# Half-tile K transposes on VectorE and small operations moved to GpSimd, in a cached-attention and MLP decode kernel

## The chip, the cores and the metric

The kernel runs on one core of a Trainium2 chip. The metric is the device time of one execution in microseconds (us); quoted times are medians of the runs of one kernel. The profile is of one such execution; its span is about 2 us shorter than the time. Engines are named as in the profile: PE is TensorE, PEld its weight loads, DVE is VectorE, ACT is ScalarE, POOL is GpSimd, SP the engine that issues the loads. The granted clock is the TensorE clock that the profile shows as granted, as a share of full speed.

## The reference, cut to what matters

```python
# x: (4, 1, 576) bf16; 32 query heads, 16 K/V heads, head size 128;
# attention over the last W = 2048 of 8192 cached keys
def reference(A_x, A_k_cache, A_v_cache, A_wq, A_wo, B_x, B_w1, B_w2, B_w3, B_w4):
    xn = layernorm(A_x)
    q = (xn @ A_wq)                                  # 2 query heads share one K/V head
    p = softmax(q @ k_window.T * 128 ** -0.5)
    attention = (p @ v_window).reshape(4, 1, 4096) @ A_wo
    # for a sequence of one token, the shifted mixer of the MLP branch adds nothing
    mlp = xn + gelu(layernorm(xn) @ B_w3) @ B_w4
    return A_x + attention + mlp
```

The work is small and the data large: for each of 16 K/V heads a K tile and a V tile of 2 MB (4 batch rows, 2048 keys, 128 channels, bf16), plus wq, wo, w3 and w4. Together the profile counts 87.17 MB on the load queue.

## The kernel before

A K tile arrives with keys on partitions, while the scores need channels there. DVE transposes it, seen as int32 (two bf16 channels at once), a quarter tile per instruction. Then PE multiplies; the softmax chain of the head before runs interleaved:

```python
def k_transpose(h, s):                     # s = 0..3, a quarter of the K tile of head h
    src = kv_tiles["K", h][:].bitcast(I32)[:, s * SC:(s + 1) * SC, :].rearrange("p c (ib i) -> p ib c i", i=QD)
    kt = ktp.tile([P, 2, SC, QD], I32, tag="kt")          # pool of 3 buffers
    nc.vector.transpose(out=kt[:], in_=src)
    kts[h, s] = kt

def sm_max(h):                             # maximum of the scores of head h
    mx = small.tile([P, 1], F32, tag="mx")
    nc.vector.reduce_max(out=mx[:], in_=S_ps[h][:], axis=AX.X)
    dm = small.tile([P, NG], BF16, tag="dm")
    nc.vector.tensor_scalar(out=dm[:], in0=sel_g[:], scalar1=mx[:, 0:1], scalar2=None, op0=ALU.mult)
    st["dm", h] = dm

def sm_maxT(h):                            # PE gathers the maxima over partitions: tile mg
    mg = ps_m.tile([NJ, NG], F32, tag="m", name="mg")
    nc.tensor.matmul(out=mg[:], lhsT=sel_jb[:], rhs=st.pop(("dm", h))[:], start=True, stop=True)
...
for t in range(Hkv):                       # hm, hv, hf, hp: heads t-1, t-2, t-3, t-4
    for s in range(NSL):                   # NSL = 4
        ...
        n = t * NSL + s + 1
        if n < Hkv * NSL:
            k_transpose(*divmod(n, NSL))   # the next quarter
        if s == 0:
            if hm >= 0:
                sm_max(hm)
            ...
            k_mask(t)
        elif s == 1 and hm >= 0:
            sm_maxT(hm)
        ...
        if hv >= 0:
            pv(hv, s)                      # probabilities times V, of head t-2
        k_scores(t, s)
```

So on PE's list stand, per head: mask, PV and scores (quarter 0), then **mg**, which needs dm, then PV and scores of quarter 1, and so on. PE takes its list in order: when dm is late, everything behind mg waits.

The loads share six K/V buffers. w4 comes last, in six pieces:

```python
W4_PIECES = [0, 10, NFH, NF - 6, NF - 2, NF - 1, NF]      # NFH = 18, NF = 36 blocks
...
mlp_out(*pieces[0]); ...; mlp_out(*pieces[1]); o_proj(hl)  # hl: the last head
mlp_out(*pieces[2]); mlp_out(*pieces[3])
... # copy one accumulator out, then pieces 4 and 5, the sum, the store
```

## Time and profile before

| | before |
|---|---|
| time, median of the first 3 runs (range) | 212.07 us (211.9 to 212.22) |
| span of the profiled run | 210.2 us |
| busy: PE, DVE, ACT, POOL | 147.2, 120.1, 33.9, 2.8 us |
| load queue, share of 16 engines' span | 97.5% |

Lines of the page of the kernel before: the busy time of the engines; then, over 40 equal slices of the span, the busy share of the DMA engines in tenths and the GB/s; then the load queue with packets, MB and share.

```profile
PE 147.2 (70%) x941; PEld 62.4 (30%) x955; DVE 120.1 (57%) x217; ACT 33.9 (16%) x64; POOL 2.8 (1%) x15
...
DMA  7999999999999999999999999999999999999991
GB/s 281 418 399 430 421 430 435 427 430 436 436 442 414 426 433 420 446 424 433 436 421 433 430 420 437 433 433 422 433 426 430 422 442 433 421 436 426 421 414 60
...
q1 hardware_dynamic: 6640, 87.17, 97.5%
```

No engine is close to full, and the DMA row is at 9 everywhere but in the first and the last slice. The kernel is bound by loading; there is no slice in which a faster engine would let loads start earlier.

Groups of DVE instructions (line, engine, operation, tile; busy us and mean ns of one; idle of DVE before them and what ended it), kernel before: the transposes, the maximum, and the product dm.

```profile
L225 DVE STREAM_TRANSPOSE kt<-kn 128x1024 int32<-128x1024 int32 x64 | 76.3, 1216 | 11.1 <-DMA kn<-in_A_k_cache_dram 10.8
L344 DVE TENSOR_REDUCE mx<-S 128x1 f32<-128x512 f32 x16 | 10.5, 657 | 1.3 <-PE S L338 1.3
...
L346 DVE TENSOR_SCALAR dm<-sel_g,mx 128x16 bf16<-128x16 bf16 x16 | 3.7, 231 | 0.6
```

What PE waited for, kernel before (us in total, times, longest us):

```profile
PE O L390 <- DMA vn<-in_A_v_cache_dram: 37.5, 10, 14.1
...
PE mg L351 <- DVE dm L346: 3.5, 3, 2.6
...
PE acc L183 <- DMA w_sb<-in_B_w_dram: 1.9, 1, 1.9
```

PE waits mostly for V tiles, hardly ever for dm. The last line is the slack of the compute: near the end PE has done everything that stands before this piece of w4 and waits 1.9 us for it. The same place in the timeline (start us, us, engine, line, what; in brackets the idle time before it and what ended it):

```profile
202.83 0.29 PE L183 MATMUL acc_odd<-wo_sb,op 128*8 128x288 bf16 x1
205.01 0.28 PE L183 MATMUL acc<-w_sb,gT 128*8 128x288 bf16 x1 [1.89 <-DMA w_sb<-in_B_w_dram]
```

### The profile page before, as it was taken

What the parts mean: (1) busy time and instruction counts of PE and PEld (TensorE: products, weight loads), DVE (VectorE), ACT (ScalarE), POOL (GpSimd) and SP (SyncE); (2) the same over time, 40 slices, a digit from 0 to 9 for tenths busy, and PEclk for the clock granted to TensorE, in tenths of its full rate; (3) what the DMA queues carried; (4) which work ended last, traced back from release to release, by engine and by line L of the source; (5) the groups of instructions that cost most, each with busy time, mean ns of one, the idle gap of its engine ahead of it and who ended that gap; (6) DMA issues with size and microseconds to landing.
All of it is one profiled execution on the core that took longest, in us unless ns stands there. A gap on an engine that the chain in (4) does not pass through costs nothing.

```text
span 210.2 us, 2389 instructions
## 1 busy us (share of the span) xinstructions
PE 147.2 (70%) x941; PEld 62.4 (30%) x955; DVE 120.1 (57%) x217; ACT 33.9 (16%) x64; POOL 2.8 (1%) x15
## 2 busy tenths in 40 slices
PE   0395694789394008849699689997883956988954
PEld 0132231224131002314154234343431321543533
DVE  4832999267831082637603879898578381593220
ACT  7603100021111000202012211220211020202300
POOL 4010000000000000000000000000000000000000
PEclk9998599589979555979699969999999695899999
DMA  7999999999999999999999999999999999999991
GB/s 281 418 399 430 421 430 435 427 430 436 436 442 414 426 433 420 446 424 433 436 421 433 430 420 437 433 433 422 433 426 430 422 442 433 421 436 426 421 414 60
DMA packets 6659, 87.32 MB, mean 415 GB/s; under 512 B 748, under 2 KB 1016, under 8 KB 1400
## 3 DMA queue, kind: packets, MB, share of 16 engines
q1 hardware_dynamic: 6640, 87.17, 97.5%
q8 instruction: 7, 0.11, 0.2%
q14 instruction: 4, 0.03, 0.0%
q10 hardware_dynamic: 8, 0.00, 0.0%
HBM read 87.17 MB, written 0.00 MB: 415 GB/s over the span
## 4 chain that ended last, share of the span: by engine, by line
DMA 65%; PE 22%; DVE 8%; issue 2%; ACT 1%; SPq 1%; DVEq 0%
DMA w_sb<-in_B_w_dram 33%; DMA vn<-in_A_v_cache_dram 26%; PE S L338 9%; DMA wq_sb<-in_A_wq_dram 6%; DVE kt L225 4%; PE O L390 3%; PE g_ps L456 2%; PE acc L183 2%; PE q_ps L285 2%; PE oT L403 1%; DVE mx L344 1%; PE S L360 1%; DVE qz L317 1%; PE gT_ps L468 1%; ACT q_sb L296 1%
## 5 line engine op out<-in xcount | busy, mean ns | idle before, releaser
L225 DVE STREAM_TRANSPOSE kt<-kn 128x1024 int32<-128x1024 int32 x64 | 76.3, 1216 | 11.1 <-DMA kn<-in_A_k_cache_dram 10.8
L338 PE MATMUL S<-kt,qz 128*128 128x512 bf16 x242 | 76.1, 437 | 5.2 <-DVE kt L225 3.1
L390 PE MATMUL O<-vn,PT 128*32 128x512 bf16 x256 | 27.9, 434 | 38.7 <-DMA vn<-in_A_v_cache_dram 37.5
L338 PEld LDWEIGHTS <-qz 128*128 128x128 bf16 x256 | 21.8, 104 | 42.0 <-issue 26.2
L366 ACT ACTIVATE E<-S 128x512 bf16<-128x512 f32 x16 | 9.5, 597 | 119.8 <-PE S L360 119.8
L390 PEld LDWEIGHTS <-PT 128*32 128x32 bf16 x256 | 7.3, 95 | 47.0 <-DVE kt L225 25.2
L372 DVE STREAM_TRANSPOSE PT<-E 128x512 bf16<-128x512 bf16 x16 | 11.4, 710 | 15.1 <-ACT E L366 15.1
L356 DVE TENSOR_REDUCE nm<-mg 8x1 bf16<-8x16 f32 x16 | 2.3, 146 | 23.0 <-PE mg L351 22.9
L397 ACT ACTIVATE O_sb<-O,rd 128x512 f32<-128x512 f32 x16 | 11.0, 686 | 16.2 <-issue 11.0
L344 DVE TENSOR_REDUCE mx<-S 128x1 f32<-128x512 f32 x16 | 10.5, 657 | 1.3 <-PE S L338 1.3
L413 DVE TENSOR_REDUCE on<-oT 128x8 bf16<-128x128 f32 x16 | 4.5, 280 | 11.1 <-PE oT L403 11.1
L403 PE MATMUL oT<-ident_w,O_sb 128*128 128x128 f32 x64 | 10.6, 291 | 0.2 <-issue 0.2
L403 PEld LDWEIGHTS oT<-ident_w,O_sb 128*128 128x128 f32 x64 | 8.6, 153 | 4.6 <-issue 2.4
L183 PE MATMUL acc<-wo_sb,op 128*8 128x288 bf16 x56 | 7.5, 286 | 0.0
L376 PEld LDWEIGHTS dn<-rs,same_j 128*128 128x128 f32 x32 | 5.8, 188 | 2.9 <-ACT E L366 0.7
L360 PE MATMUL S<-nm,j_row 8*128 8x512 bf16 x16 | 6.6, 410 | 0.0
L183 PE MATMUL acc<-w_sb,gT 128*8 128x288 bf16 x38 | 5.1, 286 | 1.9 <-DMA w_sb<-in_B_w_dram 1.9
L329 PE MATMUL S<-negbig,ohT 4*128 4x512 bf16 x16 | 6.2, 385 | 0.2 <-issue 0.2
L351 PE MATMUL mg<-dm,sel_jb 128*8 128x16 bf16 x16 | 2.8, 174 | 4.0 <-DVE dm L346 3.5
L183 PEld LDWEIGHTS <-op 128*8 128x8 bf16 x64 | 4.6, 87 | 2.4 <-issue 0.3
L456 PE MATMUL g_ps<-w_sb,ln2T 128*32 128x512 bf16 (+1 forms) x50 | 5.3, 480 | 0.0
L351 PEld LDWEIGHTS <-sel_jb 128*8 128x8 bf16 x16 | 1.3, 83 | 12.7 <-issue 6.8
(93 smaller groups left out, 80.0 us busy)
## 6 DMA issues: line engine op xcount, KB each, us to landing
kn<-in_A_k_cache_dram SPq DMA_DIRECT2D x16, 2048.0 KB, 22.3
vn<-in_A_v_cache_dram SPq DMA_DIRECT2D x16, 2048.0 KB, 24.8
wo_sb<-in_A_wo_dram SPq DMA_DIRECT2D x4, 1152.0 KB, 25.5
w_sb<-in_B_w_dram SPq DMA_DIRECT2D x1, 4608.0 KB, 35.8
wq_sb<-in_A_wq_dram SPq DMA_DIRECT2D x1, 4096.0 KB, 12.4
w_sb<-in_B_w_dram SPq DMA_DIRECT2D x1, 1728.0 KB, 33.6
w_sb<-in_B_w_dram SPq DMA_DIRECT2D x1, 1440.0 KB, 27.8
w_sb<-in_B_w_dram SPq DMA_DIRECT2D x2, 576.0 KB, 33.8
```

The costliest lines, as they stand in the source:

```text
L183: nc.tensor.matmul(out=to[q:q + OR, :], lhsT=lhsT[:, NI - 1 - i:NI - 1 - i + OR], rhs=rhs[:, i * CW:(i + 1) * CW], start=start, stop=False ...
L225: nc.vector.transpose(out=kt[:], in_=src)
L329: nc.tensor.matmul(out=S_ps[h][:].rearrange("p (c k) -> p c k", k=QD), lhsT=ohT[:], rhs=negbig[:].unsqueeze(1).to_broadcast([B, SC, QD]), ...
L338: nc.tensor.matmul(out=S_ps[h][:], lhsT=qz[:, z0:z0 + P], rhs=kt[:, ib, :, e:2 * QD:2].rearrange("p c k -> p (c k)"), start=False, stop=Fa ...
L344: nc.vector.reduce_max(out=mx[:], in_=S_ps[h][:], axis=AX.X)
L360: nc.tensor.matmul(out=S_ps[h][:], lhsT=j_row[:], rhs=st.pop(("nm", h))[:, 0:1].to_broadcast([NJ, NW]), start=False, stop=False, skip_grou ...
L366: nc.scalar.activation(out=E[h][:].rearrange("p c k -> p (c k)"), in_=S_ps.pop(h)[:], func=ACT.Exp, scale=scale, accum_out=rs[:])
L372: nc.vector.transpose(out=PT[h][:], in_=E.pop(h)[:])
L390: nc.tensor.matmul(out=O_ps[h][g * QD:(g + 1) * QD], lhsT=PT[h][:, c, :], rhs=vn[:, :, c, :], start=(s == 0), stop=False, skip_group_check ...
L397: nc.scalar.activation(out=O_sb[h][:], in_=O_ps.pop(h)[:], func=ACT.Copy, scale=st.pop(("rd", h))[:, 0:1])
L403: nc.tensor.transpose(out=oT[:, s, :], in_=o[:, s, :], identity=ident_w[:, s * NJ:s * NJ + P])
L456: nc.tensor.matmul(out=g_ps[g * QD:(g + 1) * QD], lhsT=ln2T[:, k, :], rhs=rhs, start=(j == 0), stop=False, skip_group_check=True)
```

## The change

Its intent is to relieve DVE: half as many transposes, each twice as large, and small work handed to the nearly idle POOL. The core of the diff:

```diff
-    ktp = ctx.enter_context(tc.tile_pool(name="kt", bufs=3))
+    ktp = ctx.enter_context(tc.tile_pool(name="kt", bufs=2))
...
-    def k_transpose(h, s):
-        src = kv_tiles["K", h][:].bitcast(I32)[:, s * SC:(s + 1) * SC, :].rearrange("p c (ib i) -> p ib c i", i=QD)
-        kt = ktp.tile([P, 2, SC, QD], I32, tag="kt")
+    def k_transpose(h, half):
+        c0 = half * 2 * SC
+        src = kv_tiles["K", h][:].bitcast(I32)[:, c0:c0 + 2 * SC, :].rearrange("p c (ib i) -> p ib c i", i=QD)
+        kt = ktp.tile([P, 2, 2 * SC, QD], I32, tag="kt")
         nc.vector.transpose(out=kt[:], in_=src)
...
-        nc.vector.tensor_copy(out=sel[:, :, :, kb, :],
+        nc.gpsimd.tensor_copy(out=sel[:, :, :, kb, :],
... (sel_jb and same_j in the same way)
-        nc.vector.tensor_scalar(out=dm[:], in0=sel_g[:], scalar1=mx[:, 0:1], scalar2=None, op0=ALU.mult)
+        nc.gpsimd.tensor_scalar(out=dm[:], in0=sel_g[:], scalar1=mx[:, 0:1], scalar2=None, op0=ALU.mult)
... (the five elementwise operations of the MLP activation: nc.vector to nc.gpsimd)
-            n = t * NSL + s + 1
-            if n < Hkv * NSL:
-                k_transpose(*divmod(n, NSL))
+            if s == 0:
+                k_transpose(t, 1)
+            elif s == 2 and t + 1 < Hkv:
+                k_transpose(t + 1, 0)
```

The tile E loses its second buffer, and k_scores picks its quarter out of the half.

More of the change, by code (lines that the diff above doesn't have):

```diff
@@ L220 @@
     kts = {}
-    def k_transpose(h, s):
-        src = kv_tiles["K", h][:].bitcast(I32)[:, s * SC:(s + 1) * SC, :].rearrange("p c (ib i) -> p ib c i", i=QD)
-        kt = ktp.tile([P, 2, SC, QD], I32, tag="kt")
+    def k_transpose(h, half):
+        c0 = half * 2 * SC
+        src = kv_tiles["K", h][:].bitcast(I32)[:, c0:c0 + 2 * SC, :].rearrange("p c (ib i) -> p ib c i", i=QD)
+        kt = ktp.tile([P, 2, 2 * SC, QD], I32, tag="kt")
         nc.vector.transpose(out=kt[:], in_=src)
-        kts[h, s] = kt
+        kts[h, half] = kt
     sel = part(4 * P).rearrange("p (i e k x) -> p i e k x", i=2, e=2, k=NQD)
     for kb in range(NQD):
-        nc.vector.tensor_copy(out=sel[:, :, :, kb, :],
+        nc.gpsimd.tensor_copy(out=sel[:, :, :, kb, :],
                               in_=ident_bf[:].rearrange("p (ib i e) -> p ib e i", ib=2, e=2))
@@ L249 @@
     sel_jb = const.tile([P, NJ], BF16)
-    nc.vector.tensor_copy(out=sel_jb[:], in_=sel_j[:])
+    nc.gpsimd.tensor_copy(out=sel_jb[:], in_=sel_j[:])
     sel_g = const.tile([P, NG], BF16)
@@ L258 @@
     same_j = const.tile([P, P], F32)
-    nc.vector.tensor_copy(out=same_j[:].rearrange("p (g j) -> p g j", j=NJ),
+    nc.gpsimd.tensor_copy(out=same_j[:].rearrange("p (g j) -> p g j", j=NJ),
                           in_=sel_j[:].unsqueeze(1).to_broadcast([P, NG, NJ]))
@@ L333, in k_scores @@
     def k_scores(h, s):
-        kt = kts.pop((h, s))[:].bitcast(BF16)
+        half, c0 = s // 2, s % 2 * SC
+        kt = kts[h, half][:].bitcast(BF16)
+        if s % 2:
+            kts.pop((h, half))
         for ie in range(4):
@@ L338, in k_scores @@
             nc.tensor.matmul(out=S_ps[h][:], lhsT=qz[:, z0:z0 + P],
-                             rhs=kt[:, ib, :, e:2 * QD:2].rearrange("p c k -> p (c k)"),
+                             rhs=kt[:, ib, c0:c0 + SC, e:2 * QD:2].rearrange("p c k -> p (c k)"),
                              start=False, stop=False, skip_group_check=True)
@@ L363, in sm_exp @@
     def sm_exp(h):
-        E[h] = ptp.tile([P, SC, QD], BF16, tag="e", name="E")
+        E[h] = ptp.tile([P, SC, QD], BF16, tag="e", name="E", bufs=1)
         rs = small.tile([P, 1], F32, tag="rs", bufs=3)
@@ L477, in mlp_act @@
         u = const.tile([P, NF, B], F32, name="g_u")
-        nc.vector.tensor_tensor(out=u[:], in0=xs[:], in1=xs[:], op=ALU.mult)
-        nc.vector.tensor_scalar(out=u[:], in0=u[:], scalar1=GELU_A, scalar2=1.0, op0=ALU.mult, op1=ALU.add)
-        nc.vector.tensor_tensor(out=u[:], in0=u[:], in1=xs[:], op=ALU.mult)
+        nc.gpsimd.tensor_tensor(out=u[:], in0=xs[:], in1=xs[:], op=ALU.mult)
+        nc.gpsimd.tensor_scalar(out=u[:], in0=u[:], scalar1=GELU_A, scalar2=1.0, op0=ALU.mult, op1=ALU.add)
+        nc.gpsimd.tensor_tensor(out=u[:], in0=u[:], in1=xs[:], op=ALU.mult)
         nc.scalar.activation(out=u[:], in_=u[:], func=ACT.Tanh, scale=GELU_C)
-        nc.vector.tensor_scalar(out=u[:], in0=u[:], scalar1=0.5, scalar2=0.5, op0=ALU.mult, op1=ALU.add)
-        nc.vector.tensor_tensor(out=gT[:, :, ROWS], in0=u[:], in1=xs[:], op=ALU.mult)
+        nc.gpsimd.tensor_scalar(out=u[:], in0=u[:], scalar1=0.5, scalar2=0.5, op0=ALU.mult, op1=ALU.add)
+        nc.gpsimd.tensor_tensor(out=gT[:, :, ROWS], in0=u[:], in1=xs[:], op=ALU.mult)
     def mlp_out(lo, hi):
```

## The prediction

> **What bounds the kernel now.** The DMA queue. The table of stretches shows a DMA share of 1.00 to 1.02 in every stretch from 13 to 205 us, at 421 to 434 GB/s; the page puts q1 at 97.5% of 16 engines' span, for 87.17 MB. The Trainium skill ("SBUF — State Buffer", section "SBUF: two separate sides") gives this path about 436 GB/s and 432 measured; this trace agrees. Bytes do not change, so loading still ends near 205 us. Then comes a tail: PE waits 1.9 us for the last piece of w4 until 205.01, then w4 matmuls, the sum and the store. Before it, PE starts its projections at 13.14, when wq lands.
>
> The engines are not the bound: PE busy 147.2 us, DVE 120.1. The chain of waits lists PE and DVE pieces (about 102 to 140 us, after the MLP), but DMA stayed full there.
>
> **What the change does (estimates from this trace).**
> - K transposes: 64 of 1.216 us become 32. A 512-element transpose takes 0.71, a 1024-element one 1.216, about 1 ns per element: 2048 should take 2.25 us. DVE saves about 5.5 us.
> - dm (16 x 0.231), selection copies (about 1.0 us together) and the activation chain (1.45 us) leave DVE for POOL. DVE busy falls from 120 to about 108 us, POOL rises to about 15. I expect dm at 0.3 to 0.6 us there.
> - Added latency: in each head the half-tile transpose stands ahead of the maximum on DVE. Today 1.22 + 0.65 + 0.23 us pass before mg; afterwards about 2.25 + 0.65 + 0.5. Where PE is not waiting for V, it will idle 1 to 2 us before mg.
> - K tiles are freed earlier, V tiles are not.
> - MLP head: the activation no longer holds DVE up, which returns about 1.5 us.
>
> **How much is critical.** Almost nothing. Heads 8 to 11 should lag today's times by up to 4 to 5 us, but I count at least 8 us of issued, unlanded loads at the tightest point (about 113 us), and the waits for V (3.2 us before 162.9, 4.4 before 175.3) absorb the lag. In the last head it is about 1.1 us at mg, plus 0.3 for dm; the slack before the last w4 piece is 1.9. So the end should hardly move. Set-up on POOL ends well before wq lands.
>
> **Prediction: 212.1 us, 8 in 10 between 211.0 and 213.4.** Faster by over 2%: 0.01; within 2%: 0.94; slower by over 2%: 0.05.
>
> **What would show each step.**
> - Saturation: DMA share about 1.00 from 13 to 205 us, last w4 landing within 1 us of 205.
> - Transposes: 32 of 2.2 to 2.3 us; DVE busy 106 to 110 us.
> - Longer maximum chain: PE idle of 1 to 2 us before mg in heads 9 to 12, released by dm; now mostly 0.2 or none.
> - Tail: PE still waits for w4, but about 0.5 us.
> - Set-up: q_ps still starts at 13.1 us.
>
> **What would make it wrong.** dm on POOL far slower than 0.6 us; PE's granted clock falling further through the new gaps (score matmuls already take 1.9 instead of 1.07 us per slice after long waits), so that the last head's lag exceeds 1.9 us and the end slips 1 to 4 us; or a lag after the MLP that drains the queue: a DMA share under 0.95 around 110 to 150 us.

## The result, and the profile after

| | before | after |
|---|---|---|
| time, median of 6 runs (range) | 212.0 us (211.9 to 212.22) | 212.47 us (212.36 to 213.43) |
| span of the profiled run | 210.2 us | 210.6 us |
| busy: PE, DVE, POOL | 147.2, 120.1, 2.8 us | 151.1, 113.2, 11.7 us |

The ratio is 1.0034, with a 95% interval from 1.0012 to 1.0056: the same within 2%, with a small loss that is clear of the noise. (A ratio here is the mean time of one kernel's fast runs over that of the other's in the same rounds, so not quite the ratio of the medians.) Executions over 1.5% slower than the fastest of the same kernel are left out of the means. The six runs after are in two groups, four at 212.4 to 212.6 and two at 213.3 to 213.4; those of before have one. (Of all 33 runs of the kernel before, the six here and those beside the experiments, one took 213.85 us.)

The page after, the same lines as above:

```profile
PE 151.1 (72%) x941; PEld 64.7 (31%) x955; DVE 113.2 (54%) x158; ACT 33.8 (16%) x64; POOL 11.7 (6%) x42
...
DMA  7999999999999999999999999999999999999991
GB/s 275 423 398 433 423 426 436 436 423 436 442 427 421 429 429 421 444 429 429 436 426 429 429 417 439 436 436 423 433 428 429 429 433 429 429 433 420 428 394 47
...
q1 hardware_dynamic: 6640, 87.17, 97.3%
```

DMA is as full as before, which is why 7 us less on DVE bought nothing. The groups after:

```profile
L226 DVE STREAM_TRANSPOSE kt<-kn 128x2048 int32<-128x2048 int32 x32 | 73.6, 2304 | 44.0 <-PE S L342 27.1
...
L350 POOL TENSOR_SCALAR dm<-sel_g,mx 128x16 bf16<-128x16 bf16 x16 | 5.2, 327 | 163.9 <-DVE rd L385 142.4
```

32 large transposes save only 2.7 us over 64 small ones (76.3 to 73.6), and DVE now idles 27.1 us before them until PE frees a kt buffer. Waits of PE after:

```profile
PE mg L355 <- POOL dm L350: 20.7, 12, 2.3
PE O L394 <- DMA vn<-in_A_v_cache_dram: 18.6, 5, 11.5
```

The wait for V has halved and a wait for dm has taken its place. PE is not working more usefully; it waits at mg and therefore reaches V later. The end of the timeline shows the slack after (what took it in this run is read in experiment 2):

```profile
204.46 0.29 PE L183 MATMUL acc<-wo_sb,op 128*8 128x288 bf16 x1
204.47 0.29 PE L183 MATMUL acc_odd<-wo_sb,op 128*8 128x288 bf16 x1
205.01 0.28 PE L183 MATMUL acc<-w_sb,gT 128*8 128x288 bf16 x1 [0.26 <-DMA w_sb<-in_B_w_dram]
```

The piece of w4 is usable at 205.01 us in both traces, to the hundredth. PE reaches it with 0.26 us to spare instead of 1.89. The output store is issued at 208.14 us in both.

Why dm is late can be read from DVE's timeline in a head where PE does not wait for V. Before:

```profile
126.03 2.33 DVE L225 STREAM_TRANSPOSE kt<-kn 128x1024 int32<-128x1024 int32 x2
128.28 0.65 DVE L344 TENSOR_REDUCE mx<-S 128x1 f32<-128x512 f32 x1
128.97 0.23 DVE L346 TENSOR_SCALAR dm<-sel_g,mx 128x16 bf16<-128x16 bf16 x1
129.11 0.16 DVE L381 RECIPROCAL rd<-dn 128x1 f32<-128x1 f32 x1
129.19 1.23 DVE L225 STREAM_TRANSPOSE kt<-kn 128x1024 int32<-128x1024 int32 x1
```

After, with the POOL and PE lines that follow:

```profile
125.74 2.31 DVE L226 STREAM_TRANSPOSE kt<-kn 128x2048 int32<-128x2048 int32 x1 [1.74 <-PE S L342]
...
127.98 0.65 DVE L348 TENSOR_REDUCE mx<-S 128x1 f32<-128x512 f32 x1
128.56 0.15 DVE L385 RECIPROCAL rd<-dn 128x1 f32<-128x1 f32 x1
128.80 0.33 POOL L350 TENSOR_SCALAR dm<-sel_g,mx 128x16 bf16<-128x16 bf16 x1 [9.60 <-DVE rd L385]
129.18 0.17 PE L355 MATMUL mg<-dm,sel_jb 128*8 128x16 bf16 x1 [1.82 <-POOL dm L350]
```

DVE sat idle until PE had finished the last scores of the head before (they free a kt buffer), at 125.74. Those scores are all that the maximum needs, too, yet it starts 2.24 us later, behind a half tile that nobody needs until quarter 2. Then come 0.65 us for mx, a step to POOL and 0.33 us for dm, and PE has been idle for 1.82 us. Before, DVE worked on two quarters while the scores were still running (they end at 127.84), and the maximum started 0.4 us after them.

### The profile page after: what moved, and what is told of

Read it like the earlier page. It is cut to its first block, busy times and chain, and to the rows that moved or that the text cites. A ratio compares the mean times of both kernels' runs of the same rounds, so it can differ in the third digit from the quotient of the medians.

```text
span 210.6 us, 2371 instructions
## 1 busy us (share of the span) xinstructions
PE 151.1 (72%) x941; PEld 64.7 (31%) x955; DVE 113.2 (54%) x158; ACT 33.8 (16%) x64; POOL 11.7 (6%) x42
## 4 chain that ended last, share of the span: by engine, by line
DMA 53%; PE 29%; DVE 12%; issue 2%; ACT 1%; SPq 1%; POOL 1%; DVEq 0%
DMA w_sb<-in_B_w_dram 31%; DMA vn<-in_A_v_cache_dram 16%; PE S L342 13%; DVE kt L226 9%; DMA wq_sb<-in_A_wq_dram 6%; PE O L394 4%; PE acc L183 3%; PE oT L407 2%; PE g_ps L460 2%; PE q_ps L286 2%; DVE mx L348 2%; PE S L364 1%; POOL dm L350 1%; PE gT_ps L472 1%; DVE qz L318 1%
## 5 line engine op out<-in xcount | busy, mean ns | idle before, releaser
L226 DVE STREAM_TRANSPOSE kt<-kn 128x2048 int32<-128x2048 int32 x32 | 73.6, 2304 | 44.0 <-PE S L342 27.1
L342 PE MATMUL S<-kt,qz 128*128 128x512 bf16 x242 | 77.3, 444 | 6.7 <-DVE kt L226 4.2
L355 PE MATMUL mg<-dm,sel_jb 128*8 128x16 bf16 x16 | 2.7, 171 | 20.7 <-POOL dm L350 20.7
L350 POOL TENSOR_SCALAR dm<-sel_g,mx 128x16 bf16<-128x16 bf16 x16 | 5.2, 327 | 163.9 <-DVE rd L385 142.4
L407 PE MATMUL oT<-ident_w,O_sb 128*128 128x128 f32 x64 | 12.4, 327 | 0.1
L407 PEld LDWEIGHTS oT<-ident_w,O_sb 128*128 128x128 f32 x64 | 9.8, 169 | 5.1 <-issue 3.5
L364 PE MATMUL S<-nm,j_row 8*128 8x512 bf16 x16 | 7.4, 461 | 0.0
L380 PEld LDWEIGHTS dn<-rs,same_j 128*128 128x128 f32 x32 | 6.3, 202 | 3.2 <-ACT E L370 0.7
```

Of the source, the lines that this page charges most:

```text
L342: nc.tensor.matmul(out=S_ps[h][:], lhsT=qz[:, z0:z0 + P], rhs=kt[:, ib, c0:c0 + SC, e:2 * QD:2].rearrange("p c k -> p (c k)"), start=False ...
L350: nc.gpsimd.tensor_scalar(out=dm[:], in0=sel_g[:], scalar1=mx[:, 0:1], scalar2=None, op0=ALU.mult)
L364: nc.tensor.matmul(out=S_ps[h][:], lhsT=j_row[:], rhs=st.pop(("nm", h))[:, 0:1].to_broadcast([NJ, NW]), start=False, stop=False, skip_grou ...
L407: nc.tensor.transpose(out=oT[:, s, :], in_=o[:, s, :], identity=ident_w[:, s * NJ:s * NJ + P])
```

## The experiments

Theory: the kernel is bound by loading; the change makes the compute chain **longer** by placing a long transpose ahead of the maximum; the loads hide that, down to the last 0.26 us of slack. Rivals: the engines already bind the kernel (as the chain of waits may suggest, the profile's list of what ended last, followed backwards: it has PE and DVE pieces); or POOL is what makes dm late.

Some kernels compute something wrong. The comparison with the reference passed them all the same, so it is too loose to tell which K or V tile a head has used, and "correct" says little about that for any kernel here.

### 1. Loads taken away: what each kernel costs when loading does not bind

Each K and V tile is loaded once and used for two heads. All compute stays; 33.6 of 87.2 MB go. The same edit was made in five kernels, called the light kernels below.

```diff
-    order = [("K", 0), ("K", 1), ("K", 2)]
-    for h in range(Hkv):
+    order = [("K", 0), ("K", 2)]
+    for h in range(0, Hkv, 2):
         order.append(("V", h))
-        if h + 3 < Hkv:
-            order.append(("K", h + 3))
+        if h + 4 < Hkv:
+            order.append(("K", h + 4))
...
         kv_tiles[kind, h] = t
+        kv_tiles[kind, h + 1] = t
... (buffers are counted free every second head; the last two wo tiles are loaded after heads 7 and 11)
```

The kernel before:

> The kernel before with each K and V tile loaded once for two heads (33.6 MB of 87.2 not loaded, wrong on purpose, all compute kept). 53.6 MB at 430 GB/s are 125 us, so the queue no longer binds. Theory: about 21 us of start, 16 heads of 7 to 7.5 us, 8 us for the MLP and 10 us at the end: 150 to 162 us. Rival (engines already bind the full kernel): hardly under 200 us.

The changed kernel:

> The changed kernel with the same loads taken away. Theory: with the queue out of the way its own cost shows. Heads take 9.5 to 10 us as in its trace between 119 and 139 us, so 180 to 195 us, 15% or more slower than the light kernel before. Rival (less VectorE work makes the chain shorter and only the queue hides it): as fast as or faster than the light kernel before.

The changed kernel with the maximum moved ahead of the transpose (its edit is in experiment 2):

> The changed kernel with the maximum ahead of the transpose, and the same loads taken away. Theory: the order was the cost, so this is within 3% of the light kernel before, 148 to 162 us. Rival (size or GpSimd is the cost): within 5% of the light changed kernel.

The kernel before with only the moves to POOL:

> The kernel before with only the moves to GpSimd (quarter transposes kept), and the same loads taken away. Theory: dm is 0.1 us longer and one hop between engines more, 0.1 to 0.3 us per head where PE waits for it, less what VectorE saves: within 3% of the light kernel before. Rival (GpSimd is the cost): over 8% slower than it.

The changed kernel with everything but the transposes back on DVE:

> Only the half-tile transposes, everything else on VectorE, with half of the K and V loads taken away: the fourth corner to the light runs of before (169.4), changed (195.9) and GpSimd only (169.0). Theory: the transposes' place is the whole cost, so 190 to 197 us. Rival (both parts are needed for it): under 180 us.

| half of the K and V loads gone | median us (range) | PE idle before mg | PE busy | mean granted clock |
|---|---|---|---|---|
| before | 169.4 (169.33 to 169.49) | 6.0 | 137.4 | 0.948 |
| GpSimd moves only | 169.04 (168.3 to 170.95) | 7.6 | 135.0 | 0.969 |
| transposes only | 185.64 (184.5 to 186.6) | 25.3 | 139.6 | 0.963 |
| changed | 195.86 (194.33 to 197.55) | 26.5 | 148.3 | 0.893 |
| changed, maximum first | 167.47 (166.92 to 167.9) | 2.7 | 136.8 | 0.957 |

(One of four runs of "GpSimd moves only" and one of "changed", the slowest of each, were slow. Their medians are of all four; the means of the fast runs are 168.8 and 195.3.)

The waits that decide it: PE's lines on mg of, in this order, the light kernels before, changed, and changed with the maximum first.

```profile
PE mg L352 <- DVE dm L347: 6.0, 10, 2.5
```

```profile
PE mg L356 <- POOL dm L351: 26.5, 15, 2.3
```

```profile
PE mg L356 <- POOL dm L351: 2.7, 2, 1.7
```

What follows. The full kernel before takes 212 us, and 169.4 without half of its K and V loads: loading was the bound, and the rival that the engines bind falls (it expected hardly under 200). With the loads out of the way, the changed kernel is 15% slower than the kernel before (195.3 over 169.4), a loss that the full kernel shows as 0.3%. Moving one call makes it good: with the maximum first it is 1% faster than the kernel before. That kernel keeps the half tiles, POOL, two kt buffers and one E buffer, so none of these is harmful by itself; the place of the transpose is. My sizes were off: I expected 150 to 162 us for the kernel before, 148 to 162 with the maximum first, and 180 to 195 for the changed one, whose median is just above that.

The two parts of the change do not add up. The transposes cost 16.2 us, the moves to POOL alone nothing (0.6 us less by the fast runs), both together 25.9 us. Theory put the whole cost on the transposes (190 to 197 us for them alone), which was too much: about 10 us need both. (The runs with the transposes only were made later than the others, on another chip; the kernel before took 212.04 us there and 211.98 here.) The spans show where these are: from transposes only (183.0) to changed (194.9) are 11.9 us, of which the idle time before mg has 1.2 and PE's busy time 8.7. PE does the same work more slowly, at a lower granted clock (0.893 against 0.963). Runs of one and the same kernel differ in this way too: transposes only took 184.5 and 184.8 us at 0.963, 186.5 and 186.6 at 0.945; the changed kernel 194.3 and 195.0 us at 0.91, 196.7 at 0.893. This last run is the profiled one, the slowest of its fast runs, so the two spans overstate the difference of the means (9.7 us). The table of stretches from 100 to 140 us (length, then busy us and instructions of PE, PEld, DVE, ACT, POOL; clock, DMA share, GB/s), light kernel before, then transposes only, then changed:

```profile
100.00:140.00 40.00, 38.44 (x246) 16.41 (x250) 35.77 (x60) 7.46 (x16) 0.00 (x0) 1.00 0.73 302
```

```profile
100.00:140.00 40.00, 33.76 (x215) 14.74 (x213) 29.80 (x38) 6.88 (x15) 0.00 (x0) 0.98 0.53 214
```

```profile
100.00:140.00 40.00, 32.09 (x185) 13.99 (x188) 25.65 (x31) 6.40 (x14) 2.85 (x8) 0.87 0.48 191
```

The typical idle time before mg there is 0.2 to 0.5 us, 1.59 us and 1.82 us, the clock 1.00, 0.98 and 0.87. That the gaps set the clock is suggested by this order, not shown: no run changed the gap alone. The Trainium skill ("TensorE: Matmul & The Clock Gate", section "What's actually happening") says that a monitor sets the share of clock pulses by how busy PE has lately been, at half rate when idle; that the granted clock falls to 0.50 in some stretches (below) agrees with the half rate; on when it falls, see the last section.

### 2. The full kernel, one part at a time

The order alone:

```diff
-            if s == 0:
-                k_transpose(t, 1)
-            elif s == 2 and t + 1 < Hkv:
+            if s == 2 and t + 1 < Hkv:
                 k_transpose(t + 1, 0)
 
             if s == 0:
                 if hm >= 0:
                     sm_max(hm)
                 if hv >= 0:
                     sm_rec(hv)
+                k_transpose(t, 1)
                 if hp >= 0:
                     o_pick(hp)
```

> The changed kernel with one thing moved: in each head the maximum of the head before stands ahead of the half-tile transpose on VectorE, not behind it. Theory (the long transpose delays the maximum, and that made PE idle 1.8 us per head before mg): PE's idle before mg falls from 20.7 us to under 5, the period of unconstrained heads from 9.9 to about 7 us, PE waits 1.5 to 2.5 us for w4 again, and the time is that of before, 211.9 to 212.2, without runs at 213.4. Rival (dm on GpSimd makes the delay): idle before mg stays above 15 us, time stays at 212.4.

The transposes alone, with dm, the copies and the activation back on DVE (nc.gpsimd to nc.vector in those lines):

> The changed kernel with every operation that had gone to GpSimd back on VectorE; only the half-tile transposes (and the order they bring) remain. Theory: most of the loss is from the transposes' place, so PE's idle before mg stays at 15 to 20 us, the wait for the last w4 is 0.3 to 0.9 us, the time is 212.0 to 212.5. Rival (GpSimd is to blame): idle before mg falls under 5 us and the wait for w4 is back at 1.9 us.

With the maximum first: 212.32 us (212.27 to 212.43), ratio 1.0015 [1.0002, 1.0027]. Transposes only: 212.08 us (211.92 to 212.77), ratio 1.0007 [0.9994, 1.0020]. PE's waits, maximum first:

```profile
PE O L394 <- DMA vn<-in_A_v_cache_dram: 36.2, 10, 15.4
...
PE mg L355 <- POOL dm L350: 2.7, 2, 1.7
PE acc L183 <- DMA w_sb<-in_B_w_dram: 1.7, 1, 1.7
```

and transposes only:

```profile
PE O L394 <- DMA vn<-in_A_v_cache_dram: 28.4, 9, 15.6
PE mg L355 <- DVE dm L350: 15.2, 9, 3.6
...
PE acc L183 <- DMA w_sb<-in_B_w_dram: 1.6, 1, 1.6
```

The order accounts for the new wait (20.7 to 2.7 us) and gives the slack back (1.7 us), as theory said. Transposes only keep the wait (15.2 us) and yet keep 1.6 us of slack; here theory expected 0.3 to 0.9. The difference lies in the last turn of the loop. There PE waits for V until 184.9 us in all three traces and then starts level. The first scores after that, before, changed and transposes only:

```profile
185.26 1.08 PE L338 MATMUL S<-kt,qz 128*128 128x512 bf16 x4
```

```profile
185.21 1.89 PE L342 MATMUL S<-kt,qz 128*128 128x512 bf16 x4
```

```profile
185.21 1.08 PE L342 MATMUL S<-kt,qz 128*128 128x512 bf16 x4
```

In the changed kernel the granted clock was 0.50 between 186 and 188 us, mg came at 187.02 without any wait for dm (before: 186.26), and the output projection that had started at 188.05 before started at 189.47. With transposes only the clock was 1.00 there, and it started at 188.32. So of the 1.6 us of slack lost in this run, 1.4 are a dip of the clock; the longer chain itself added 0.2 us, at the last mg (a wait of 0.94 us for dm, 0.72 before). That the change caused this dip is not shown: similar dips stand in traces of experiments 3 and 4 whose kernels have quarter transposes or the maximum first. One of the five runs with transposes only took 212.77 us, at a mean clock of 0.871 instead of 0.894; it has no trace.

The time with the maximum first did not come back to that of before, by 0.3 us, although nothing in its trace is late: the store is issued at 208.18 us. Its times are 2.1 us above its spans, those of before 1.8. For the changed kernel the store is issued at 208.14, as before, and the span ends 0.4 us later. What takes these tenths, before the span or after the store, is open; both kernels have small operations on POOL, while transposes only, without them, came out at the time of before. No run tested it.

### 3. The last V tile not loaded: how much slack there is

Head 15 uses the V tile of head 14, so that 2.1 MB, 4.9 us at 430 GB/s, are missing just before w4.

```diff
     for h in range(Hkv):
-        order.append(("V", h))
+        if h < Hkv - 1:
+            order.append(("V", h))
...
         kv_tiles[kind, h] = t
+        if (kind, h) == ("V", Hkv - 2):
+            kv_tiles["V", Hkv - 1] = t
```

> The kernel before, but head 15 reuses the V tile of head 14, so that 2.10 MB (4.9 us of the DMA queue) are not loaded; the result is wrong on purpose. Theory (queue bound, compute of the last heads starts when V of head 13 lands and has 1.9 us of slack before w4): w4 lands 4.9 us earlier, but the compute chain from V 13 to the last output projection is unchanged, so the time falls by that slack only, 1.5 to 2.2 us, to about 210.1. Rival A (the PE and DVE pieces of the chain of waits bound the kernel): no change, 212. Rival B (the queue alone counts, no compute chain close behind it): 4.9 us less, 207.

> The same removal in the changed kernel. Theory: its compute chain has used up all but 0.26 us of the slack, so the time falls by 0.1 to 0.6 us only, to about 212.0, some 1.6 us above the run of the kernel before without that tile. Rival A: no change. Rival B: 4.9 us less, 207.5.

Before: 210.51, 210.62, 212.24 and 212.30 us, in two groups. Changed: 212.58 once, and 213.95 to 214.15 three times. That loading alone counts (4.9 us less) is refuted: right behind it stands the compute chain of the last heads. The faster group of each kernel (two runs, and one) is near what theory expected, 1.4 to 1.5 us less and no gain, and the two differ by 2.0 us. The other group was not expected, and over all four runs the gain of the kernel before is not clear of the noise (ratio 0.9971 [0.9936, 1.0006]; changed 1.0074 [1.0043, 1.0105]). The profiled run of each kernel fell in it; from the table of stretches of the kernel before without that tile (columns as above):

```profile
194.00:196.00 2.00, 1.54 (x18) 0.73 (x18) 0.72 (x5) 0.67 (x2) 0.00 (x0) 1.00 1.03 438
196.00:198.00 2.00, 1.86 (x22) 0.75 (x18) 0.88 (x3) 0.70 (x2) 0.00 (x0) 0.71 0.95 406
198.00:200.00 2.00, 2.00 (x16) 0.92 (x10) 0.20 (x1) 0.69 (x1) 0.00 (x0) 0.50 0.97 390
200.00:202.00 2.00, 1.93 (x24) 1.16 (x21) 0.12 (x2) 0.00 (x0) 0.00 (x0) 0.93 0.44 167
202.00:204.00 2.00, 1.69 (x30) 1.16 (x31) 1.11 (x3) 0.00 (x0) 0.00 (x0) 1.00 0.00 0
```

Loading is over at 202 us, and PE, slowed to half its clock between 198 and 200 us, sets the end. The last output projection starts at 203.64, against 201.97 in the kernel before. The last mg was late by only 0.1 us (194.43 against 194.33), so this dip of the clock costs about 1.6 us. In the full kernel before, 1.9 us of slack would cover it; with 0.26 us of slack it would show. That fits the two groups of runs after, 1 us apart, but no trace of a 213.4 us run was taken, nor of the one run of the kernel before at 213.85.

The trace of the changed kernel without the tile has a dip of the same size at 199 to 201 us, so the two can be set side by side. mg of the last loop turn comes at 186.38 before and at 187.64 in the changed kernel, after 1.49 us of waiting for dm; the last output projection starts at 203.64 and 205.08, the store is issued at 207.76 and 209.20. Here the longer chain itself costs 1.4 us at the end.

### 4. Finer pieces of w4: can the slack be turned into time?

PE waits until 205.01 us for the third of the six pieces, and then has 18 blocks to do. If that piece came as three, part of the blocks could be done before.

```diff
-    W4_PIECES = [0, 10, NFH, NF - 6, NF - 2, NF - 1, NF]
+    W4_PIECES = [0, 10, NFH, 22, 26, NF - 6, NF - 2, NF - 1, NF]
...
-    mlp_out(*pieces[2])
-    mlp_out(*pieces[3])
+    for lo, hi in pieces[2:-2]:
+        mlp_out(lo, hi)
...
-    for lo, hi in pieces[4:]:
+    for lo, hi in pieces[-2:]:
```

> The kernel before, with the third piece of w4 (12 blocks, 1.7 MB) loaded as three pieces of 4. PE now waits until 205.01 us for that piece and then has 18 blocks of 0.12 us left; with finer pieces 8 of the 18 can be done before 205.0. Theory (after the last load only PE's remaining blocks count): 0.7 to 1.0 us less, 211.0 to 211.4. Rival (the landing of the very last pieces bounds the end): under 0.2 us.

> The same split in the changed kernel, whose compute reaches w4 only at about 204.7 us. Theory of the lost slack: it cannot use the earlier pieces, so it gains under 0.4 us and ends at 212.0 to 212.6, 0.7 us or more above the kernel before with the split. Rival (its slack does not matter): it gains as much as the kernel before does.

> Half-tile transposes with the maximum ahead of them, all operations on VectorE, and the split of w4. Theory: it has the slack back (1.7 us in the run with the maximum first), so it gains what the kernel before gains: 211.0 to 211.4. Rival: the half tile itself costs slack, 211.6 or more.

Before with fine pieces: 212.16 us (212.0 to 212.21), ratio 0.9996 [0.9971, 1.0021]. Maximum first, all on DVE, fine pieces: 212.24 us (211.94 to 212.32), ratio 0.9999 [0.9973, 1.0024]. Changed with fine pieces: 213.63 us (212.34 to 213.77), ratio 1.0055 [1.0022, 1.0088].

No gain: my theory of the end was wrong. The timeline of the kernel before with fine pieces shows a second wait:

```profile
205.01 0.28 PE L183 MATMUL acc<-w_sb,gT 128*8 128x288 bf16 x1 [0.77 <-DMA w_sb<-in_B_w_dram]
...
206.40 0.28 PE L183 MATMUL acc<-w_sb,gT 128*8 128x288 bf16 x1 [0.74 <-DMA w_sb<-in_B_w_dram]
```

The next piece, of blocks 30 to 33, is usable only at 206.40 us, and no wait for the last two pieces, of one block each, follows: the landing of the last pieces bounds the end, as the rival had it. Until now PE's remaining blocks had hidden that. After 205 us the queue runs down, and the piece that I had called the last was the third. (The run at 213.85 us of the kernel before is one of those taken beside these three kernels and widens the three intervals; without it the first ratio is 1.0004.) No kernel of this study that loads everything beats the one before.

The changed kernel suffers where the two others do not. I expected at most 212.6 us, with no use of the finer pieces but no harm either. Five of its six runs are at 213.6 to 213.8; its profile has this stretch, and its last w4 blocks run until about 208.7 us without any wait for a load:

```profile
186.00:188.00 2.00, 0.38 (x6) 0.18 (x5) 1.97 (x6) 0.00 (x0) 0.33 (x1) 0.95 1.01 434
188.00:190.00 2.00, 2.00 (x9) 0.81 (x6) 0.04 (x1) 0.00 (x0) 0.00 (x0) 0.50 1.01 434
190.00:192.00 2.00, 2.00 (x14) 1.26 (x13) 0.29 (x1) 0.00 (x0) 0.00 (x0) 0.70 0.99 426
```

PE idles before mg (0.38 of 2 us busy; 1.62 us of it waiting for dm), and mg comes at 187.67, 1.4 us later than in the kernel before with fine pieces (186.24). Then the clock falls to 0.50, and the output projection is 2.8 us late (190.82 against 188.02), more than the slack; the end slips 1.5 us. The kernel with the maximum first also had a dip to 0.50, at 198 to 200 us, and still ended at 212.15 in that run: it had slack to spend. This is the clearest sight of what the change gave away.

## Why the prediction was right

The forecast was 212.1 us, in a range of 211.0 to 213.4; measured were 212.47 us, the same within 2%.

- **Loading is the bound, and it ends when it did.** Right. DMA share is 0.99 to 1.02 in stretches of 15 to 20 us from 13 to 205 us, and the awaited w4 piece is usable at 205.01 in both traces. The light kernels show it by force: 33.6 MB fewer take 42.6 us off the kernel before. The Trainium skill ("SBUF — State Buffer", section "SBUF: two separate sides") has 436 GB/s for the step from DMA to SBUF, and the stretches of the changed kernel from 13 to 190 us run at 429 to 434.
- **Transposes of 2.2 to 2.3 us, DVE saves 5.5 us on them, busy 106 to 110.** The duration was 2.304 us, at the edge; the saving was mis-sized, 2.7 us instead of 5.5, and DVE's busy time is 113.2. I took the fixed cost of an instruction from two sizes of different types (0.71 us for 512 bf16, 1.216 for 1024 int32). Where two quarters follow one another directly, nearly nothing is saved: the pair takes 2.33 us in the timeline and a half tile 2.31, since the end of one instruction overlaps with the start of the next. The Trainium skill ("Perfetto Trace Analysis", section "Optimizing Scalar/DVE Operations") describes such an overlap: an overhead of about 60 ns per DVE instruction on SBUF, of which the profile shows about twice as much, half of it overlapped. By durations a merged pair saves 2 x 1216 - 2304 = 128 ns, which agrees with the doubled figure.
- **dm takes 0.3 to 0.6 us on POOL.** Right, 0.327. POOL's busy time of about 15 us was an overestimate; it is 11.7.
- **PE idles 1 to 2 us before mg.** Right: 20.7 us over 12 heads, typically 1.82. But the prediction named heads 9 to 12; it is in nearly every head in which PE does not wait longer for V.
- **The lag grows to 4 to 5 us and is absorbed.** Nearly right in size: mg of head 11 comes 5.2 us later than before (159.56 against 154.39), and 0.3 us later two heads on (177.96 against 177.71). The queue was not drained.
- **In the tail 1.1 + 0.3 of 1.9 us are used, 0.5 us remain.** 0.26 us remain. That the number is near is luck in this run. The step that was to use the slack, the longer chain, added only 0.2 us here; a dip of PE's clock, which the sum does not hold, took 1.4 (experiment 2). In the traces of experiments 3 and 4 the chain's own lag is 1.3 to 1.4 us at mg, close to the 1.4 predicted, and a dip comes on top. I had named that dip among what could make the prediction wrong; the runs at 213.4 may be such a case, which is not shown.
- **Set-up.** Right: PE's projections start at 13.07 us.
- **Not seen:** that the piece of w4 which PE awaits is not the last, and that the final loads are usable only at about 206.4 us. This did not matter for the forecast, but it made experiment 4 fail.

What the prediction gave too little weight is that the change is a loss to the compute, of about 26 us, which loading hides, and not merely a change without effect.

## What to carry to other kernels

When the load queue is full from end to end, judge a change to the compute by the slack it leaves before the last loads, or by a copy of the kernel with part of the loads taken away: there a loss of 15% showed that the full kernel reported as 0.3%. On an engine that works in order, what another engine waits for must stand ahead of long work that is needed later; merging two instructions makes that work twice as long and saved little here: 2.33 us became 2.31 back to back. The Trainium skill ("Perfetto Trace Analysis", section "Optimizing Scalar/DVE Operations") has the rule for it, that breaking instructions up may let work finish sooner when the engine is not saturated but makes others wait, and the light kernels agree with it (169.4 us with quarters, 185.6 with halves). But moving one call did as much with the halves left whole (167.5 us).

## What the Trainium skill lacked or had wrong

- "TensorE: Matmul & The Clock Gate": its table ties a return to half rate to idle windows of about 3.4 us; further down the page tells of a kernel whose clock went back and forth because PE idled briefly and often, without saying how briefly or how often. Here the granted clock fell to 0.50 with waits much shorter than 3.4 us: in the kernel before without the last V tile at 198 to 200 us, when PE's longest listed wait since 181 us was 0.9 us; and the light changed kernel, with 1.82 us of idle time before mg per head of some 10 us, ran at 0.87 on average between 100 and 140 us. What sets these dips is open. They matter: PE is busy 8.7 us longer in the light changed kernel, at a mean clock of 0.893, than with the transposes only, at 0.963.
- "Perfetto Trace Analysis": it gives one overhead for all DVE instructions on SBUF and their overlap, but no duration of a transpose. Here: 64 of 1216 ns against 32 of 2304 ns, and 2.33 us for two small ones in a row against 2.31 us for one large.
- "GPSIMD Engine Reference" has no duration for a product of a small tile with a scalar per partition. Here it took 0.327 us on POOL for 128 x 16 bf16, against 0.231 us on DVE.
